# Second pair of batches in another order of groups: where a fused attention and two-layer MoE kernel makes its weight differences

## The chip, the cores and the metric

One core of a Trainium2 chip runs the whole program in one launch. The metric is the device time of one execution in microseconds (us), taken as the median of several runs. Five engines work side by side, each through its own instructions in order: TensorE (PE; PEld is its weight load), VectorE (DVE), ScalarE (ACT), GpSimd (POOL) and SyncE (SP). The last two only issue DMAs here.

## The reference

```
x:      4 batches, 8 heads, 512 rows, 64 wide;   state: 4 batches, 8 heads, 32 rows, 64 wide
a  = softmax(x state^T / 8);     xread = a  state
a2 = softmax(state x^T / 8);     sread = a2 x
y  = [xread; sread], as 4 * 544 tokens of width 512
y  = (h - tanh(h)) w_out           with h = y  w_in     (512 -> 2048 -> 512)
out = (h * tanh(softplus(h))) w_out2  with h = y w_in2   (512 -> 2048 -> 512)
```

The weights come as float64 and are converted by the kernel; all else is float32.

## The kernel before

To keep float32 precision every operand of a product is split into a large and a small part (`h` and `l` in the names), and a product is three matmuls (`mm3p`): large by large, large by small, small by large. A split is one ScalarE rounding (`gh<-...`, `wh<-...`) and one VectorE subtraction (`gl<-...`, `wl<-...`).

The change lies in the second MoE layer. Its 2048 hidden columns are taken in 8 **groups** of 256, and the four batches in two **pairs**: first batches 0 and 1 through groups 0 to 7, then batches 2 and 3 through groups 0 to 7. Within a group the product y times w_in2 over the pair is computed with Strassen's scheme in Winograd's form: seven products (`product`, names m1, m6, m7, m2, m5, m3, m4 in this order) of six matmuls each, into three PSUM banks a, b and c (`UB`). VectorE adds between them (`plus`): p after m6, then q and h22 after m5, h12 after m3, h21 after m4. m6, m5 and m3 all write bank b, so m5 needs p done, and **m3 needs q done**. ScalarE applies the activation (`mish`).

After each product stands a `slot`: it runs one item from `fill` (work of the group before, so that TensorE has matmuls while VectorE adds), then a callback, then one step from the queue `soon`, one or two weight loads from `ahead` (issued by SP), and some background `pieces`. For the first pair the items of `fill` are `down_2`: one of 8 output tiles of g times w_out2, six matmuls and one addition on VectorE (`out<-acc,out`).

For groups 0 to 5 of the second pair the second product uses Winograd's scheme too, with two groups summed in PSUM: 15 items (`pair_items`) per pair of groups, whose operands are the sums s1 to s4 of g (`a_sum`) and the **differences** t1 to t4 of w_out2. The differences do not depend on the batch. They are made once per group by `forms_t`, in the slots of the first pair's next group: two additions `wv<-wo`, four half-width subtractions `tf<-...` and two splits (`wh<-tf` on ScalarE, `wl<-tf` on VectorE), which is eight VectorE and two ScalarE steps, and four stores by POOL (`wt<-...`). `load_forms` reads them back for the second pair (`wf<-wt`). `prep` splits the left operand of an item ahead of it.

In the first pair's groups 1, 2, 3 and 7 background **pieces** run as well: the last conversions of w_in2 and w_out2 and the preparation of the second pair's y (`pieces_y`). Groups 6 and 7 of the second pair are taken plainly (`down_2`). In the last group the seven Winograd sums are added up into the outputs by `combos`: six steps of VectorE additions, one step per slot, so that the following `down_2` items can add to them.

Each engine's order is fixed by the order in which the Python code calls it (`Pinned`, whose call stands at line 66, so that nearly all rows of the profile carry L66).

```
        slot(min(u + g, 1), lambda: mish_lo(*c22))
        product(u, g, "m3", b, False)
        free_w("s34")
        h12 = plus(b, m1, m1)
```

Of the kernel before, what the change touches and what calls it, by code (L numbers as in the profile page):

```python
# [30 lines left out]
AHEAD = (2, 6, 10)  # L31
QUARTERS = 2


# [44 lines left out]
def attention_moe_kernel(  # L79
# [151 lines left out]
    def split(src, n=512, name="s", by=0):  # L231
# [17 lines left out]
    D2O = [dram.tile([128, 2, 512], F32, tag=f"o{t}", name="wo") for t in range(NT)]  # L249
    D2T = [  # L250
        dram.tile([128, 4, 2, 256], F32, tag=f"t{g}", name="wt") for g in range(NT // 2 - 2)
    ]

# [663 lines left out]
    def product(u, g, m, bank, start):  # L917
        x, op = LEFT[m]
        for k in range(KH):
            yh, yl = YB[u, RIGHT[m], k]  # L920
            mm3p(
                bank, w2(g, x, k, 0, op), w2(g, x, k, 1, op), yh.t, yl.t,
                start and k == 0, k == KH - 1, skip_group_check=not start,
            )
        if g == NT // 2 - 1:
            for k in range(KH):
                put(*YB.pop((u, RIGHT[m], k)))
# [33 lines left out]
    def mish_lo(key, u, h):  # L961
        if h is None:
            G2[key] = u
# [60 lines left out]

    def group(u, g, fill, ahead, with_s, rate, whole=False, keep=0, per=1, end=None):


        a, b, c = (psum.tile([128, 512], F32, tag=t, name="h") for t in UB)
        more = rate + (rate > 1)

        def slot(pieces, *after):
            for _ in range(per):
                if len(fill) > keep:
                    f = fill.popleft()
                    if f:
                        f()
            for f in after:
                f()
            if soon:
                soon.popleft()()  # L1040
            for _ in range(1 if whole else 2):
                if ahead:
                    ahead.popleft()()
            background(pieces, 0)
# [42 lines left out]
    def downs(u, g, with_s, last=False):  # L1087
# [4 lines left out]
        done = []  # L1092
        make = forms_t(g) if u == 0 and g < len(D2T) else []

# [11 lines left out]

    waiting = []

    def forms_t(g):


        v = {}

        def whole(j):
            h, l = O2[2 * g + j]
# [33 lines left out]

        def first():  # L1150
            whole(0)

        def release():
            put(*waiting)
            del waiting[:]

        return [
            first, lambda: whole(1), lambda: sums(0, 1), lambda: sums(2, 3),
            lambda: keep(0), lambda: keep(1), lambda: None, release,
        ]  # L1160

# [7 lines left out]
    USES = {"a11": 3, "a12": 2, "a21": 2, "a22": 2, "s1": 2, "s2": 2, "s3": 1, "s4": 1}  # L1169
    AF, GS, WF, PG, R, left = {}, {}, {}, {}, {}, {}  # L1170
    sdown = []
# [17 lines left out]
    def take_group(g):  # L1189
        for name, key in AFORM.items():  # L1190
            own(g, name, G2.pop(key))
        GS[g] = G2.pop("s")
# [49 lines left out]
    def pair_items(pair):  # L1242
        def item(i, hh):
            name, form_a, form = PORDER[i]
            if name == "s":
                s_part(pair, form)
                if pair[0] == 0:
                    OUT["s", 0] = get("out")
# [18 lines left out]
            if hh and form in BFORM:  # L1267
                s_part(pair, form)
            if pair[0] == 0:
                R[name, hh] = get("r")  # L1270
# [16 lines left out]
    def combos(b):  # L1287
# [15 lines left out]

        def one(hh):
            into(hh, "p6", "p1")
            to_out(hh, b, 0, "p1", "p2")
            put(R.pop(("p1", hh)), R.pop(("p2", hh)))

        def two(hh):
            into(hh, "p7", "p6")  # L1310
            into(hh, "p6", "p5")
            to_out(hh, b + 1, 0, "p7", "p4", ALU.subtract)
            put(R.pop(("p4", hh)))

        def three(hh):
            to_out(hh, b, 1, "p6", "p3")
            to_out(hh, b + 1, 1, "p7", "p5")
            put(*(R.pop((x, hh)) for x in ("p3", "p5", "p6", "p7")))

        return [lambda f=f, hh=hh: f(hh) for hh in range(2) for f in (one, two, three)]  # L1320

    def loads_in(g):
        g %= NT // 2
        return deque(
# [235 lines left out]
    fill = [lambda q=q: down(q) for q in seq[low:]]  # L1560
    groups = [(u, g) for u in range(2) for g in range(NT // 2)]
    for j, (u, g) in enumerate(groups):
        ahead = loads_out(g) if u == 0 or g >= NT // 2 - 2 else deque()
        if j + 1 < len(groups):
            ahead += loads_in(g + 1)
        if u and g == 0:
            background(len(bg), 0)
        if (u, g) == (0, 2):
            background(len(bg), 0)
# [4 lines left out]
            bg.extend(pieces_ys() + later[:EARLY])  # L1574
        elif (u, g) == (0, NT // 2 - 1):
            bg.extend(later[EARLY:])
        rate = 2 if g == NT // 2 - 1 or u == 0 and g < 2 else 1
        fill = deque(fill)
        if u == 0 or g >= NT // 2 - 2:
            if u and g == NT // 2 - 1:  # L1580
                soon.extend(combos(2 * u))
                first = list(fill)
                fill = deque([None] * 3 + first[:2] + first[4:5] + first[2:4] + first[5:])
            group(u, g, fill, ahead, u == 1, rate, per=2 if u and g == NT // 2 - 2 else 1)
            fill = downs(u, g, u == 1, j + 1 == len(groups))
            continue
        pair = (g - g % 2, g - g % 2 + 1)
        if g % 2:
            ahead.extend([lambda i=i, p=pair: load_forms(p, i) for i in range(2)])
            group(  # L1590
                u, g, fill, ahead, True, rate, True, 0, 1,
                lambda p=pair: (take_group(p[1]), prep(p, 0)),
            )
            fill = pair_items(pair)
        else:
            if g == 0:
                first = list(fill)
                fill = deque(
                    [None] * 2 + first[:4] + [None] * 3 + first[4:]
                )  # L1600
            group(
                u, g, fill, ahead, True, rate, True, len(fill) - 7, 1,
                lambda p=pair: take_group(p[0]),
            )
# [35 lines left out]
```

## Time and profile before

| what | value |
|---|---|
| three runs, median (lowest to highest) | 714.44 us (713.74 to 714.95) |
| the profiled execution | 716.0 us, its span 714.2 us |
| TensorE busy | 694.8 us, 97% of the span |
| VectorE busy | 516.0 us, 72% |
| ScalarE busy | 367.8 us, 51% |
| chain of waits, by engine | TensorE 81%, VectorE 9%, ScalarE 7%, issue 2%, DMA 1% |
| granted TensorE clock | full speed (2.4 GHz) in all 40 slices of the span |

The profile is one execution; its times count from the start of the span. A row of the timeline has the start, the length, the engine, the line, the operation with what it writes and reads, and in brackets the idle time of the engine before it with the instruction that ended it. Matmuls overlap: a row of a 128x512 matmul is 0.39 us long, but the next one starts 0.23 us after it, and a matmul's recorded end is modelled.

### The profile page before, as it was taken

The numbers are of one execution on the slowest core, as the hardware profiler recorded it, in microseconds if no ns is written. First come the engines' busy times: TensorE is split into PE (matmuls) and PEld (weight loads), VectorE is DVE, ScalarE is ACT, GpSimd is POOL, SyncE is SP. The second block draws the span as 40 slices with busy tenths as digits, with TensorE's granted clock in tenths as the row PEclk, the third lists the DMA queues.
The fourth block names the chain that finished last, engine by engine and source line by source line (L and its number), as shares of the span: only waits on it lengthen the run. The fifth ranks groups of instructions, "written<-read, shape, count | busy, mean of one in ns | idle before, by whom it ended". The sixth has DMA issues, their size and how long they took to land.

```text
span 714.2 us, 11308 instructions
## 1 busy us (share of the span) xinstructions
PE 694.8 (97%) x4166; PEld 565.0 (79%) x4166; DVE 516.0 (72%) x906; ACT 367.8 (51%) x667; POOL 88.0 (12%) x134
## 2 busy tenths in 40 slices
PE   9899999999999999999999889999999999999988
PEld 6467777788777897778877678888887999999966
DVE  5799966887578757996577887767656436676774
ACT  6899645565676666776265332334424544342330
POOL 0000000125012414403023111011000000000000
PEclk9999999999999999999999999999999999999999
DMA  9976130228263657847868545676945456566203
GB/s 289 330 259 227 60 47 15 89 89 289 88 210 110 248 192 246 313 150 249 326 208 289 176 133 191 227 235 219 336 137 178 134 148 192 156 213 216 66 0 134
DMA packets 69800, 132.36 MB, mean 185 GB/s; under 512 B 16752, under 2 KB 27248, under 8 KB 69744
## 3 DMA queue, kind: packets, MB, share of 16 engines
q1 hardware_dynamic: 59504, 98.06, 42.4%
q0 software_dynamic: 10240, 33.56, 12.9%
q8 instruction: 33, 0.54, 0.3%
q14 instruction: 23, 0.19, 0.1%
HBM read 95.68 MB, written 35.91 MB: 184 GB/s over the span
## 4 chain that ended last, share of the span: by engine, by line
PE 81%; DVE 9%; ACT 7%; issue 2%; DMA 1%; DVEq 0%; ACTq 0%
PE acc L66 44%; PE h L66 30%; DVE wide L66 2%; PE hs L66 2%; PE swp L66 2%; ACT r L66 2%; ACT w L66 2%; DVE gl L66 1%; ACT gh L66 1%; ACT wide L66 1%; DVE out L66 1%; DMA wide<-in_moe_w_out_dram 1%; DVE tf L66 1%; DVE wl L66 1%; PE xtp L66 1%
## 5 line engine op out<-in xcount | busy, mean ns | idle before, releaser
L66 PE MATMUL h<-yh,ws 128*128 128x512 f32 x448 | 157.0, 394 | 7.7 <-DVE wide L66 5.4
L66 PEld LDWEIGHTS h<-yh,ws 128*128 128x128 f32 x448 | 84.3, 188 | 27.9 <-DVE wide L66 8.7
L66 PE MATMUL acc<-wo,gh 128*128 128x512 f32 (+1 forms) x332 | 101.8, 388 | 2.4 <-DVE out L66 1.9
L66 PE MATMUL acc<-gh,wh 128*128 128x512 f32 x244 | 98.5, 403 | 0.0
L66 PE MATMUL acc<-gh,wl 128*128 128x512 f32 x244 | 95.4, 391 | 0.0
L66 PE MATMUL acc<-gl,wh 128*128 128x512 f32 x244 | 95.2, 390 | 0.0
L66 PE MATMUL h<-yl,ws 128*128 128x512 f32 x224 | 87.8, 392 | 0.0
L66 DVE TENSOR_TENSOR gl<-wide,gh 128x512 fp32r<-128x512 f32 x80 | 54.0, 688 | 43.8 <-ACT gh L66 43.6
L66 ACT ACTIVATE wide<-wide 128x512 f32<-128x512 f32 x41 | 25.9, 632 | 100.4 <-DVE wide L66 100.4
L66 PEld LDWEIGHTS acc<-wo,gh 128*128 128x128 f32 x332 | 61.8, 188 | 16.0 <-DVE out L66 2.8
L66 PE MATMUL acc<-wf,gh 128*128 128x256 f32 x384 | 70.6, 283 | 0.6 <-ACT gh L66 0.6
L66 DVE TENSOR_TENSOR wide<-h,wide 128x512 f32<-128x512 f32 x78 | 53.7, 688 | 21.6 <-PE h L66 10.9
L66 PE MATMUL acc<-wo,gl 128*128 128x512 f32 (+1 forms) x166 | 64.5, 388 | 0.0
L66 PEld LDWEIGHTS acc<-wf,gh 128*128 128x128 f32 x384 | 61.8, 192 | 3.4 <-ACT gh L66 1.0
L66 PEld LDWEIGHTS acc<-gh,wh 128*128 128x128 f32 x244 | 45.8, 188 | 18.2 <-issue 4.2
L66 PE MATMUL acc<-wf,gl 128*128 128x256 f32 x192 | 54.6, 284 | 0.2 <-DVE gl L66 0.2
L66 PE MATMUL h<-ath,swh 128*128 128x512 f32 x128 | 51.6, 403 | 2.4 <-ACT swh L66 2.3
L66 PEld LDWEIGHTS acc<-gh,wl 128*128 128x128 f32 x244 | 45.8, 188 | 9.9
L66 PEld LDWEIGHTS acc<-gl,wh 128*128 128x128 f32 x244 | 45.9, 188 | 9.1 <-issue 0.4
L66 ACT ACTIVATE gh<-wide 128x512 fp32r<-128x512 f32 x80 | 48.9, 628 | 7.6 <-DVE wide L66 6.4
L66 ACT ACTIVATE wide<-h 128x512 f32<-128x512 f32 x40 | 23.7, 594 | 55.1 <-PE h L66 52.8
L66 PE MATMUL h<-ath,swl 128*128 128x512 f32 x128 | 50.6, 395 | 0.5 <-DVE swl L66 0.5
(215 smaller groups left out, 1289.1 us busy)
## 6 DMA issues: line engine op xcount, KB each, us to landing
ws<-wi SPq DMA_DIRECT2D x128, 256.0 KB, 4.5
st<-in_moe_w_in_dram SPq DMA_DIRECT2D x26, 512.0 KB, 5.1
st<-in_moe_w_out_dram SPq DMA_DIRECT2D x23, 512.0 KB, 5.2
wo<-wo SPq DMA_DIRECT2D x40, 256.0 KB, 4.0
wi<-wh POOLq DMA_DIRECT2D x32, 256.0 KB, 4.5
wi<-wl POOLq DMA_DIRECT2D x32, 256.0 KB, 4.4
wf<-wo SPq DMA_DIRECT2D x24, 256.0 KB, 4.0
wf<-wt SPq DMA_DIRECT2D x24, 256.0 KB, 4.9
```

Source lines behind the costliest of these rows:

```text
L66: i = fn(*args, **kw)
```

## The change

- The second pair takes the groups in the order of `ROUND2`, (3, 4, 5, 7, 6, 2, 0, 1); its first six (`WHOLE`) are taken with Winograd's second product in pairs (3, 4), (5, 7), (6, 2), and the last two, 0 and 1, plainly.
- The differences of w_out2 for groups 3, 4, 5 and 7 are made with the first pair's output items as before, which is in the first pair's groups 4, 5, 6 and in the second pair's first group. Those for groups 6 and 2 are made by steps in `soon` in the second pair's first and third group, from large and small parts of w_out2 that are loaded a second time (`more_t`: four DMAs of 256 KB each). In the first pair's groups 1, 2 and 3, none are made.
- The split of the first left operand of each pair of groups (`prep(p, 0)`) moves from after m4 to after m3 (`mid`).
- In the seventh group four of the 15 pair items are kept back (every second slot takes two) for the first four slots of the last one, and `combos` is cut into eight steps with one empty, which with the last four pair items in front stretches over nine slots.

```
+ROUND2 = (3, 4, 5, 7, 6, 2, 0, 1)
+WHOLE = 6
...
-        if g == 0:
+        if g == 0 and b in (0, 1):
             OUT[b, r] = get("out")
             evac(OUT[b, r].t, ps, r)
             return
         o = OUT[b, r]
-        if g < NT // 2 - 1:
+        if g != (NT // 2 - 1 if b in (0, 1) else ROUND2[-1]):
...
-            for _ in range(per):
+            done[0] += 1
+            for _ in range(2 if done[0] - 1 in per else 1):
...
-        slot(rate, lambda: mish_lo(*c12))
+        slot(rate, lambda: mish_lo(*c12), *([mid] if mid else []))
...
-        make = forms_t(g) if u == 0 and g < len(D2T) else []
+        make = forms_t(g, [O2[2 * g], O2[2 * g + 1]]) if u == 0 and g in ROUND2[:4] else []
...
+    def more_t(g):
+        src = []
+
+        def load():
+            for t in (2 * g, 2 * g + 1):
+                src.append(tuple(get("wo", F32R) for _ in range(2)))
+                for h in range(2):
+                    nc.sync.dma_start(out=src[-1][h].t.bitcast(F32), in_=D2O[t][:, h, :])
+
+        made = forms_t(g, src)
+
+        def second():
+            made[1]()
+            put(*src[0], *src[1])
+
+        return load, [made[0], second, *made[2:]]
...
-        return [lambda f=f, hh=hh: f(hh) for hh in range(2) for f in (one, two, three)]
+        return [
+            u2, u3, lambda: second(0), u4, lambda: second(1), lambda: None,
+            lambda: first(0), lambda: first(1),
+        ]
...
-    groups = [(u, g) for u in range(2) for g in range(NT // 2)]
+    groups = [(0, g) for g in range(NT // 2)] + [(1, g) for g in ROUND2]
...
+            load, steps = more_t(ROUND2[4])
+            ahead.append(load)
...
+            if n == WHOLE:
+                fill = deque(fill)
+                group(u, g, fill, ahead, True, rate, keep=4, per=(0, 2, 4, 6))
+                fill = list(fill) + downs(u, g, True)
+            else:
+                soon.extend(combos(2 * u))
+                first = fill[4:]
+                fill = deque(fill[:4] + first[:2] + first[4:5] + first[2:4] + first[5:])
+                group(u, g, fill, ahead, True, rate)
+                fill = downs(u, g, True, True)
+            continue
+        if n == 0:
+            soon.extend(steps)
+            fill = [None] * 2 + fill[:4] + [None] * 3 + fill[4:]
+            load, steps = more_t(ROUND2[5])
+        elif n == 1:
+            ahead.append(load)
+        elif n == 2:
+            soon.extend(steps)
...
             group(
-                u, g, fill, ahead, True, rate, True, 0, 1,
-                lambda p=pair: (take_group(p[1]), prep(p, 0)),
+                u, g, fill, ahead, True, rate, True, 0, (), lambda p=pair: prep(p, 0),
+                lambda g=g: take_group(g),
             )
```

In the new `combos`, u2 adds p1 to p6, u3 adds p6 to p7 and u4 adds p5 to p6, for both halves hh of the rows; `second(hh)` writes the outputs of batch 3 and `first(hh)` those of batch 2, four half-width additions each.

**VectorE in the first pair's group 2.** The rows lead up to q, the last of each list (`wide<-h,wide`); `wide<-acc` and `out<-acc` add output items, `wide<-y`, `yl` are pieces, `gl` is a split of g. Before:

```order
L66 TENSOR_TENSOR wide<-acc,wide 128x512
L66 TENSOR_TENSOR wv<-wo 128x512
L66 TENSOR_TENSOR wide<-y 128x512 x2
L66 TENSOR_TENSOR wide<-acc,wide 128x512
L66 TENSOR_TENSOR tf<-wv 128x256
L66 TENSOR_TENSOR tf<-wv,tf 128x256
L66 TENSOR_TENSOR yl<-y,yh 128x512
L66 TENSOR_TENSOR out<-acc,out 128x512
L66 TENSOR_TENSOR tf<-wv 128x256
L66 TENSOR_TENSOR tf<-tf,wv 128x256
L66 TENSOR_TENSOR gl<-wide,gh 128x512
L66 TENSOR_TENSOR wide<-h,wide 128x512
```

and now:

```order
L68 TENSOR_TENSOR wide<-acc,wide 128x512
L68 TENSOR_TENSOR wide<-y 128x512 x2
L68 TENSOR_TENSOR wide<-acc,wide 128x512
L68 TENSOR_TENSOR yl<-y,yh 128x512
L68 TENSOR_TENSOR out<-acc,out 128x512
L68 TENSOR_TENSOR gl<-wide,gh 128x512
L68 TENSOR_TENSOR wide<-h,wide 128x512
```

The `wv` and the four `tf` are gone; the rest stands in the same order.

**VectorE in the second pair's third group**, now, from after p to q and h22 (`gl<-hs,gh` is the split of the state rows; the `gl` before it that of a left operand, `m_5657` a copy of m1):

```order
L68 TENSOR_TENSOR gl<-wide,gh 128x512 x2
L68 TENSOR_TENSOR wv<-wo 128x512
L68 TENSOR_TENSOR tf<-wv 128x256
L68 TENSOR_TENSOR tf<-wv,tf 128x256
L68 TENSOR_TENSOR gl<-wide,gh 128x512 x2
L68 TENSOR_TENSOR tf<-wv 128x256
L68 TENSOR_TENSOR tf<-tf,wv 128x256
L68 TENSOR_TENSOR gl<-hs,gh 128x256
L68 TENSOR_TENSOR wide<-h,m_5657 128x512
L68 TENSOR_TENSOR wide<-h,wide 128x512
```

Before, none of the `wv` and `tf` rows stand there; the pair of `tf` in front of `gl<-hs,gh` is new directly ahead of q.

**VectorE in the last group**, before, from h12 to the remaining output additions (`out` rows of half width are steps of `combos`, the second `wide<-h,wide` is h21):

```order
L66 TENSOR_TENSOR wide<-h,wide 128x512
L66 TENSOR_TENSOR out<-acc,out 128x512
L66 TENSOR_TENSOR gl<-wide,gh 128x512
L66 TENSOR_TENSOR out<-r 128x256 x2
L66 TENSOR_TENSOR out<-r,wide 128x256 x2
L66 TENSOR_TENSOR wide<-h,wide 128x512
L66 TENSOR_TENSOR out<-acc,out 128x512
L66 TENSOR_TENSOR gl<-wide,gh 128x512
L66 TENSOR_TENSOR out<-acc,out 128x512 x13
L66 TENSOR_TENSOR out<-acc,out 128x256 x2
```

and now:

```order
L68 TENSOR_TENSOR wide<-h,wide 128x512
L68 TENSOR_TENSOR out<-acc,out 128x512
L68 TENSOR_TENSOR gl<-wide,gh 128x512
L68 TENSOR_TENSOR wide<-h,wide 128x512
L68 TENSOR_TENSOR out<-acc,out 128x512
L68 TENSOR_TENSOR gl<-wide,gh 128x512
L68 TENSOR_TENSOR out<-wide 128x256 x2
L68 TENSOR_TENSOR out<-wide,r 128x256 x2
L68 TENSOR_TENSOR out<-acc,out 128x512
L68 TENSOR_TENSOR out<-r 128x256 x2
L68 TENSOR_TENSOR out<-r,wide 128x256 x2
L68 TENSOR_TENSOR out<-acc,out 128x512 x13
```

Four half-width additions stood between h12 and h21; now eight stand behind h21, in two lots, among the additions of the output items. Ahead of q the two full-width additions of u4 stand now where one full-width and two half-width ones stood.

## Rows read from the trace of the kernel before

**Rows 1.** The page's first part: busy time of each engine.

```profile
PE 694.8 (97%) x4166; PEld 565.0 (79%) x4166; DVE 516.0 (72%) x906; ACT 367.8 (51%) x667; POOL 88.0 (12%) x134
```

**Rows 2.** Stretches: from:to, length, busy us (instructions) by engine, clock, DMA share, GB/s.

```profile
357.00:428.00 71.00, 63.77 (x274) 50.74 (x274) 56.18 (x98) 34.40 (x59) 16.46 (x25) 1.00 0.60 200
...
511.00:544.00 33.00, 33.00 (x160) 27.74 (x159) 16.74 (x27) 8.35 (x15) 0.00 (x0) 1.00 0.54 183
...
672.00:715.00 43.00, 36.38 (x169) 29.42 (x167) 27.80 (x52) 6.39 (x11) 0.00 (x0) 0.99 0.16 56
```

**Rows 3.** Timeline of PE, first pair: m6's start in groups 1, 4 and 5.

```profile
360.25 0.39 PE L66 MATMUL h<-yh,ws 128*128 128x512 f32 x1
...
430.51 0.39 PE L66 MATMUL h<-yh,ws 128*128 128x512 f32 x1
...
451.33 0.39 PE L66 MATMUL h<-yh,ws 128*128 128x512 f32 x1
```

**Rows 4.** Timeline of PE, first pair: m3's start in groups 1 and 2.

```profile
372.60 0.50 PE L66 MATMUL h<-yh,ws 128*128 128x512 f32 x1 [1.31 <-DVE mt L66]
...
398.13 0.50 PE L66 MATMUL h<-yh,ws 128*128 128x512 f32 x1 [2.98 <-DVE wide L66]
```

**Rows 5.** Timeline of DVE, first pair's group 2, up to q (the last row).

```profile
391.72 0.69 DVE L66 TENSOR_TENSOR wv<-wo 128x512 f32<-128x512 f32 x1
392.32 1.29 DVE L66 TENSOR_TENSOR wide<-y 128x512 f32<-128x512 f32 x2
...
394.13 0.42 DVE L66 TENSOR_TENSOR tf<-wv 128x256 f32<-128x256 f32 x1
...
394.92 0.69 DVE L66 TENSOR_TENSOR yl<-y,yh 128x512 fp32r<-128x512 f32 x1
...
396.12 0.42 DVE L66 TENSOR_TENSOR tf<-wv 128x256 f32<-128x256 f32 x1
...
396.79 0.68 DVE L66 TENSOR_TENSOR gl<-wide,gh 128x512 fp32r<-128x512 f32 x1
397.39 0.68 DVE L66 TENSOR_TENSOR wide<-h,wide 128x512 f32<-128x512 f32 x1
```

**Rows 6.** Timeline of PE, second pair's third group: from m1 to after m6.

```profile
544.06 0.62 PE L66 MATMUL h<-yh,ws 128*128 128x512 f32 x2
...
546.42 0.50 PE L66 MATMUL acc<-wf,gh 128*128 128x256 f32 x2 [0.61 <-ACT gh L66]
...
548.68 0.40 PE L66 MATMUL h<-yh,ws 128*128 128x512 f32 x1
...
551.50 0.40 PE L66 MATMUL h<-yh,ws 128*128 128x512 f32 x1
```

**Rows 7.** Timeline of DVE, second pair's first group, the item before m5.

```profile
520.77 0.69 DVE L66 TENSOR_TENSOR wide<-acc,wide 128x512 f32<-128x512 f32 x1 [2.03 <-PE acc L66]
```

**Rows 8.** Timeline of PE, second pair: m3 in its first and third group.

```profile
523.53 0.39 PE L66 MATMUL h<-yh,ws 128*128 128x512 f32 x1
...
562.33 0.40 PE L66 MATMUL h<-yh,ws 128*128 128x512 f32 x1
```

**Rows 9.** Timeline of DVE, second pair's third group: q.

```profile
561.48 0.68 DVE L66 TENSOR_TENSOR wide<-h,m 128x512 f32<-128x512 f32 x1
```

**Rows 10.** Timeline of PE, last group: m3 and two of the output items.

```profile
683.55 0.50 PE L66 MATMUL h<-yh,ws 128*128 128x512 f32 x1 [0.60 <-DVE wide L66]
...
693.53 0.73 PE L66 MATMUL acc<-wo,gh 128*128 128x512 f32 x2 [1.52 <-DVE out L66]
...
695.59 0.73 PE L66 MATMUL acc<-wo,gh 128*128 128x512 f32 x2 [0.39 <-DVE out L66]
```

**Rows 11.** Timeline of SP, from the end of the first pair.

```profile
501.82 8.02 SPq L905 DMA_DIRECT2D ws<-wi  x14
...
518.76 6.03 SPq L1010 DMA_DIRECT2D out_dram<-wide  x3
```

**Rows 12.** DMA issues of the stretch 485 to 550 us: count, size, median us to landing.

```profile
wo<-wo SPq DMA_DIRECT2D x3, 256.0 KB, 3.8
```

More of the change, by code (lines that the diff above doesn't have):

```diff
@@ L249, in attention_moe_kernel @@
     D2O = [dram.tile([128, 2, 512], F32, tag=f"o{t}", name="wo") for t in range(NT)]
-    D2T = [
-        dram.tile([128, 4, 2, 256], F32, tag=f"t{g}", name="wt") for g in range(NT // 2 - 2)
-    ]
+    D2T = {
+        g: dram.tile([128, 4, 2, 256], F32, tag=f"t{g}", name="wt") for g in ROUND2[:WHOLE]
+    }
     def store_split(w, dst):
@@ L962, in mish_lo @@
         if h is None:
-            G2[key] = u
+            own(whole_g[0], ANAME[key], u)
             return
@@ L1023, in plus, with group @@
         return o
-    def group(u, g, fill, ahead, with_s, rate, whole=False, keep=0, per=1, end=None):
+    def group(u, g, fill, ahead, with_s, rate, whole=False, keep=0, per=(), mid=None, end=None):
         a, b, c = (psum.tile([128, 512], F32, tag=t, name="h") for t in UB)
+        whole_g[0] = g
+        done = [0]
         more = rate + (rate > 1)
         def slot(pieces, *after):
-            for _ in range(per):
+            done[0] += 1
+            for _ in range(2 if done[0] - 1 in per else 1):
                 if len(fill) > keep:
@@ L1169, in attention_moe_kernel @@
     USES = {"a11": 3, "a12": 2, "a21": 2, "a22": 2, "s1": 2, "s2": 2, "s3": 1, "s4": 1}
-    AF, GS, WF, PG, R, left = {}, {}, {}, {}, {}, {}
+    ANAME = {key: name for name, key in AFORM.items()}
+    AF, GS, WF, PG, R, left, whole_g = {}, {}, {}, {}, {}, {}, [0]
     sdown = []
@@ L1246, in item @@
                 s_part(pair, form)
-                if pair[0] == 0:
+                if pair[0] == ROUND2[0]:
                     OUT["s", 0] = get("out")
@@ L1268, in item @@
                 s_part(pair, form)
-            if pair[0] == 0:
+            if pair[0] == ROUND2[0]:
                 R[name, hh] = get("r")
@@ L1302, in into, with u2, u3, u4 @@
             add(R[o, hh].t, R[o, hh].t, R[x, hh].t)
-        def one(hh):
-            into(hh, "p6", "p1")
-            to_out(hh, b, 0, "p1", "p2")
[L1307 to L1315, printed above, removed]
-            to_out(hh, b, 1, "p6", "p3")
-            to_out(hh, b + 1, 1, "p7", "p5")
-            put(*(R.pop((x, hh)) for x in ("p3", "p5", "p6", "p7")))
-        return [lambda f=f, hh=hh: f(hh) for hh in range(2) for f in (one, two, three)]
+        def u2():
+            for hh in range(2):
+                into(hh, "p6", "p1")
+        def u3():
+            for hh in range(2):
+                into(hh, "p7", "p6")
+        def u4():
+            for hh in range(2):
+                into(hh, "p6", "p5")
+        def second(hh):
+            to_out(hh, b + 1, 0, "p7", "p4", ALU.subtract)
+            to_out(hh, b + 1, 1, "p7", "p5")
+            put(R.pop(("p7", hh)), R.pop(("p4", hh)))
+        def first(hh):
+            to_out(hh, b, 0, "p1", "p2")
+            to_out(hh, b, 1, "p6", "p3")
+            put(*(R.pop((x, hh)) for x in ("p1", "p2", "p3", "p5", "p6")))
+        return [
+            u2, u3, lambda: second(0), u4, lambda: second(1), lambda: None,
+            lambda: first(0), lambda: first(1),
+        ]
     def loads_in(g):
-        g %= NT // 2
         return deque(
@@ L1574, in attention_moe_kernel @@
             bg.extend(pieces_ys() + later[:EARLY])
-        elif (u, g) == (0, NT // 2 - 1):
+        elif (u, n) == (0, last_g):
             bg.extend(later[EARLY:])
-        rate = 2 if g == NT // 2 - 1 or u == 0 and g < 2 else 1
-        fill = deque(fill)
[L1579 to L1588, printed above, removed]
+            load, steps = more_t(ROUND2[4])
+            ahead.append(load)
+        rate = 2 if n == last_g or u == 0 and n < 2 else 1
+        fill = list(fill)
+        if u == 0:
+            group(u, g, deque(fill), ahead, False, rate)
+            fill = downs(u, g, False)
+            continue
+        if plain:
+            if n == WHOLE:
[8 more added lines that the diff above has]
+                fill = downs(u, g, True, True)
+            continue
+        if n == 0:
[6 more added lines that the diff above has]
+            soon.extend(steps)
+        pair = ROUND2[n - n % 2:n - n % 2 + 2]
+        fill = deque(fill)
+        if n % 2:
             ahead.extend([lambda i=i, p=pair: load_forms(p, i) for i in range(2)])
             group(
-                u, g, fill, ahead, True, rate, True, 0, 1,
-                lambda p=pair: (take_group(p[1]), prep(p, 0)),
+                u, g, fill, ahead, True, rate, True, 0, (), lambda p=pair: prep(p, 0),
+                lambda g=g: take_group(g),
             )
@@ L1595, in attention_moe_kernel @@
         else:
[L1596 to L1600, printed above, removed]
             group(
-                u, g, fill, ahead, True, rate, True, len(fill) - 7, 1,
-                lambda p=pair: take_group(p[0]),
+                u, g, fill, ahead, True, rate, True, len(fill) - 7, (), None,
+                lambda g=g: take_group(g),
             )
```

31 lines of the change are left out of this document (13 added, 18 removed).

## The prediction

> **What bounds the kernel now.** I read the page's busy times first, then the stretches, then the timelines of TensorE and VectorE around each place where TensorE stands idle. TensorE is busy 694.8 of the 714.2 us [rows 1], and the change takes away none of its matmuls, so all that can be won is its 19.4 us of idle time, and of that only what lies where the change works. The stretches show where [rows 2]: the first pair's groups 1 to 3 have 71.00 - 63.77 = 7.2 us of idle, the second pair's first two groups (511 to 544) none, the close from 672 on 43.00 - 36.38 = 6.6, part of it the store after the last matmul. VectorE is at 56.18 of 71 us in the first of these, and only at 16.74 of 33 in the second. So one place has too much VectorE work and another has room.
>
> Who waits for whom is in the timeline: in groups 1 to 3, m3 begins late and its releaser is VectorE [rows 4]; VectorE itself runs without a pause up to q, the addition that frees bank b for m3 [rows 5]. A 128x512 matmul begins 0.23 us after the one before though its row lasts 0.39, so an idle time in brackets costs 0.16 more than it says: the wait of 2.98 us at 398.13 costs 3.1. A product of six such steps takes 1.36 us, an output item as much.
>
> The granted clock is 1.00 in the stretches up to 672 [rows 2], the level of 2.4 GHz, through waits of 3 us too; neither a gain nor a loss comes from the clock.
>
> **Part 1: no differences in the first pair's groups 1 to 3.** From m6 of group 1 to m6 of group 4 it takes 430.51 - 360.25 = 70.26 us; the next group, which makes differences but has no pieces, takes 451.33 - 430.51 = 20.82 [rows 3]. At that pace three groups take 62.5, so 7.8 us are lost to having both. VectorE sheds, per group, ahead of q: two `wv` at 0.60 from start to start (391.72 to 392.32), and two pairs of `tf`, 0.79 (394.13 to 394.92) and 0.67 (396.12 to 396.79) [rows 5], 2.66 us together; behind q two more `wl`, 1.2, and ScalarE two `wh`.
> - Group 2: VectorE reaches q at 397.39 [rows 5]. Without 2.66 it is 394.7, and m3 would start at 395.5 in place of 398.13, still 0.5 late. But group 1 has lost its differences as well, and the two `wl` each waited there for a `wh` behind an activation. I followed the queue from there item by item with the durations of these rows: VectorE is then bound by the items it adds, q ends 0.3 us ahead of m3's turn, and the wait is gone.
> - Group 1: q is 1.3 late [rows 4]; 2.66 us less in front brings it to within 0.1 or 0.2 us of m3's turn, held by a ScalarE step in between. Group 3, a wait of the same kind, ends with half a microsecond to spare.
> Were the small waits of the groups without pieces gone as well (0.3 each), it would be 8.7 us; I take 8.2, between 7.8 and 8.7, because of the rest in group 1. The bound from below is 0, should the pieces alone hold VectorE up.
>
> **Part 2: the first split sooner.** In the second pair's third group the first pair item waits for its left operand: from m1 (second of the two steps of the row at 544.06, so 544.29) to m6 (548.68) it takes 4.39 us, from m6 to m7 (551.50) 2.82 for the same kind of work [rows 6]: 1.57 lost. The split now stands one product and one item earlier (2.8 us), more than the wait, and no more than four steps are put in front of h21, which m7 of the next group needs some 7 us later. I take the whole 1.6; the bounds are 0.6 (the first wait's size, should the second step still wait) and 1.6.
>
> **Part 3: where the differences go.** Nothing is saved in sum: the same eight VectorE, two ScalarE steps and four POOL stores per group, and eight loads of 256 KB more on SP.
> - Second pair's first group: group 7's come with the items, group 6's from `soon`. Behind the item at 520.77 now stand `wv` and two `tf`, 0.60 and 0.67, ahead of the state split (0.34) and q. So q starts at 520.77 + 0.61 + 0.60 + 0.67 + 0.34 = 522.99 [rows 5, 7], ends at 523.68, and m3, which started at 523.53 [rows 8], comes 0.2 late; with the slow first step after a wait 0.3. Behind q the splits delay h12 and h21 by some 2 us, but those free banks for the next group's m6 and m7, later still. Second group: 0.
> - Third group: the `tf` pair right ahead of q, 0.67, puts it from 561.48 to 562.15, its end to 562.85, and m3 from 562.33 [rows 8, 9] to 562.9. With the slow step 0.7.
> - Groups 4 to 6 of the first pair are as before, and the other order of the groups alone changes no work on any engine. POOL's stores land long before they are read, a pair of groups later.
> I take 1.0 lost, between 0 (if VectorE reaches q earlier than I think) and 2.5 (if every one of the first three groups waits as long as the third).
>
> By the Trainium skill, VectorE: DVE Perf Modes, section "The DRAIN you can't avoid", the next VectorE instruction does not start until the pipe is empty; by that each of these steps would hold the queue for its whole row, 0.69 or 0.42 us. [rows 5] differ: rows of 0.69 follow each other by 0.60 and rows of 0.42 by 0.34, so the queue is priced by steps. By the rule the pair of `tf` would cost 0.84 in place of 0.67, and this part 1.4 in place of 1.0.
>
> **Part 4: the close.** Before, the last group lost 0.60 + 1.52 + 0.39 plus 0.16 each, 3.0 us [rows 10]. The order now: ahead of q, behind the split of the first activation, stand u4's two additions (1.2) where there stood 0.6 + 0.67, so about the same; but between m2 and m5 TensorE now has only the short last pair item (0.7 us) in place of an output item (1.36). The chain behind m2 (activation 0.6, rounding 0.6, split 0.6, u4 1.2, state split 0.3, q 0.7, and hand-overs of 0.2) is 4.3 us; TensorE's cover (0.7 + 0.1 + 1.36 + 1.36) is 3.6. m3 is late by some 0.8, as before. Then the eight half-width additions of batch 2 (8 x 0.34 = 2.7) stand behind h21, among the additions that free the banks of the output items; before, half of the comparable work was done ahead of h21. Following banks and queue step by step I get waits of 1.9 and 0.6 where there were 1.7 and 0.55. So the close loses 0.4; bounds: 3.0 won, if the spread leaves VectorE abreast of the items, and 2 lost, if a third item waits.
>
> **The sum.** 8.2 + 1.6 - 1.0 - 0.4 = 8.4 us less for the span of 714.2, some 705.8. The profiled execution took 716.0 with 1.8 us around the span; the median of the runs is 714.44, 1.6 less than it. I take the difference from the median: 714.44 - 8.4 = **706.0 us**. A difference under 0.2%, 1.4 us, could not be told from none.
>
> **The rivals.**
> - *The pieces, not the differences, hold the first groups.* If VectorE and ScalarE, which hand pieces and activations to each other in turn, stay late at q without the differences, part 1 gives about half, 4.1, and the time is 710.1. For it: the longest wait is in group 2, which has the most pieces; against: the steps removed ahead of q are 2.66 us of a wait of 2.98.
> - *The close keeps up.* If the additions spread over nine slots leave VectorE abreast, its 3.0 us go and the 0.4 isn't lost: 702.6. Against: no slot between m3 and the end loses VectorE work, the last two gain it.
> - *The second loads are late.* `wv` of group 6 stands at VectorE's queue head in the first slot of the second pair's first group, about 513.6, and p, q and all additions wait behind it. SP issues its loads ahead of the last twelve weight loads of the burst that fills 501.82 to 509.84 [rows 11], and such a load lands in 3.8 us [rows 12], so about 508. It decides from about 519 on, where m5 needs p; beyond that each microsecond is one lost. If SP put them behind the stores from 518.76, which wait for VectorE's additions [rows 11], they would land near 530 and the time would be some 716.5: slower than before.
> - *Bank b is what lacks.* m6, m5 and m3 write bank b in turn, and if the time from m5's end through q is what m3 waits for, less VectorE work ahead of q changes nothing: part 1 is 0, the other parts leave 714.44 - 1.6 + 1.0 + 0.4 = 714.2, the same. Against: for the same bank the wait is 1.31 us in one group and 2.98 in the next [rows 4], and none is named in groups 4 to 6. The Trainium skill, Perfetto Trace Analysis, section "Optimization Strategy", says that a gap that repeats can mean too little PSUM for the next tile; by that rule this rival would hold, and the unequal waits do not agree with it.
>
> **How the numbers follow.** The forecast (704.5 to 708) 0.66, the pieces 0.18, the close 0.08, late loads 0.04, bank b 0.04. The likeliest is 706.0. The range takes in the bound of half a gain and all but the far end of the close, 703.6 to 710.0; it leaves out late loads, bank b and part of the close. Faster by over 0.2%: 0.91, with a little taken off the cases for mechanisms that I do not see; within 0.2%: 0.05; slower: 0.04.
>
> **What would show it.** In the new profile: m3 of the first pair's groups 2 and 3 without a bracket, and 62 to 63 us from m6 of group 1 to m6 of group 4; no idle time ahead of the first `acc<-wf,gh`; small waits of 0.1 to 0.6 us for VectorE at m3 in the second pair's first and third group; in the last group again three waits that add up to some 3.3. I am wrong if groups 1 to 3 still lose over 3 us, if a DMA is named as a releaser of VectorE around 513, or if the close changes by over 1.5.

## The result, and the profile after

The changed kernel took **705.09 us** (median of four runs, 704.84 to 706.41) beside 714.39 us of the kernel before on the same chip: ratio 0.9874, with a 95% interval of 0.9857 to 0.9891. That is 9.3 us less; the prediction was 706.0, a gain of 8.4. On a second chip it was 704.97 beside 715.25, ratio 0.9859 (0.9845 to 0.9872). The profiled execution took 705.0 us, with a span of 703.2.

The page's first part, which answers to [rows 1]:

```profile
PE 692.0 (98%) x4166; PEld 563.9 (80%) x4166; DVE 515.6 (73%) x906; ACT 366.7 (52%) x667; POOL 88.0 (13%) x134
```

The instructions are as many as before on every engine, and TensorE's idle time fell from 19.4 to 703.2 - 692.0 = 11.2 us. The same stretches as in [rows 2]:

```profile
357.00:428.00 71.00, 71.00 (x315) 58.61 (x314) 53.24 (x86) 32.73 (x56) 9.13 (x14) 1.00 0.56 186
511.00:544.00 33.00, 32.98 (x173) 28.05 (x172) 24.47 (x43) 12.05 (x24) 5.80 (x8) 1.00 0.87 285
672.00:715.00 43.00, 26.09 (x119) 21.00 (x117) 19.21 (x36) 3.79 (x6) 0.00 (x0) 0.99 0.16 55
```

In the first, TensorE no longer idles at all (63.77 before), with VectorE at 53.24 in place of 56.18. These stretches hold the same times but not quite the same work, as the changed kernel is ahead. So here is the first one by work, from m6 of group 1 to m6 of group 4, before and now:

```profile
360.25:430.51 70.26, 63.02 (x272) 50.17 (x270) 56.41 (x97) 32.81 (x57) 17.80 (x26) 1.00 0.62 208
359.15:420.44 61.29, 61.29 (x272) 50.60 (x270) 46.67 (x75) 30.65 (x52) 9.13 (x14) 1.00 0.62 203
```

VectorE's share went only from 80% to 76%, and the waits are gone. In the second stretch, VectorE went from 16.74 to 24.47; what TensorE lost there is in the table below.

Now TensorE's timeline at the places of [rows 3, 4, 6, 8, 10]: m6, m3 and m3 of the first pair's groups 1, 1 and 2, m6 and m3 of group 4; m3 of the second pair's first group; m1, the first pair item and m6 of its third group, and m3; m3 and two output items of the last group.

```profile
359.15 0.39 PE L68 MATMUL h<-yh,ws 128*128 128x512 f32 x1
...
370.04 0.39 PE L68 MATMUL h<-yh,ws 128*128 128x512 f32 x1
...
390.44 0.42 PE L68 MATMUL h<-yh,ws 128*128 128x512 f32 x1
...
420.44 0.39 PE L68 MATMUL h<-yh,ws 128*128 128x512 f32 x1
...
431.61 0.50 PE L68 MATMUL h<-yh,ws 128*128 128x512 f32 x1
...
513.46 0.50 PE L68 MATMUL h<-yh,ws 128*128 128x512 f32 x1
...
534.14 0.61 PE L68 MATMUL h<-yh,ws 128*128 128x512 f32 x2
...
535.73 0.40 PE L68 MATMUL acc<-wf,gh 128*128 128x256 f32 x2
...
537.16 0.40 PE L68 MATMUL h<-yh,ws 128*128 128x512 f32 x1
...
551.36 0.50 PE L68 MATMUL h<-yh,ws 128*128 128x512 f32 x1 [0.40 <-DVE wide L68]
...
671.30 0.50 PE L68 MATMUL h<-yh,ws 128*128 128x512 f32 x1 [0.56 <-DVE wide L68]
...
682.66 0.50 PE L68 MATMUL acc<-wo,gh 128*128 128x512 f32 x1 [1.55 <-DVE out L68]
...
684.60 0.73 PE L68 MATMUL acc<-wo,gh 128*128 128x512 f32 x2 [0.29 <-DVE out L68]
```

m1 of the third group begins with the second step of its row, 534.37. The m3 at 513.46 begins 0.40 after the matmul before it, so 0.18 late, and slow steps behind it cost 0.16 more: from m1 of this group to m1 of the next it takes 17.01 us, 16.67 before. The m3 at 551.36 loses its bracket, 0.16, and 0.10 more in a slow step behind it. So the 11.0 us between the two spans are accounted for, term by term:

| place | before | after | won |
|---|---|---|---|
| up to the first pair's group 0 (both programs alike) | 334.38 | 333.29 | 1.09, chance |
| m6 of group 1 to m6 of group 4 | 70.26 | 61.29 | 8.97 |
| m6 of group 4 to m1 of the second pair's first group | 80.43 | 80.25 | 0.18 |
| m1 to m6 in the second pair's third group | 4.39 | 2.79 | 1.60 |
| at m3 and behind it, second pair's first and third group | 0 | 0.34 + 0.66 | -1.00 |
| last group, three waits with 0.16 each | 2.99 | 2.88 | 0.11 |

The change itself thus gave 8.97 + 0.18 + 1.60 - 1.00 + 0.11 = 9.86 us in the trace, between the 9.3 and 10.3 of the medians on the two chips.

VectorE's timeline shows the same from its side. First the split of g and q in the first pair's group 2 [rows 5], then the second pair's first group (`wv` from the second load; then q with h22 in one row), then the third group:

```profile
389.03 0.68 DVE L68 TENSOR_TENSOR gl<-wide,gh 128x512 fp32r<-128x512 f32 x1
389.63 0.68 DVE L68 TENSOR_TENSOR wide<-h,wide 128x512 f32<-128x512 f32 x1
...
503.11 0.68 DVE L68 TENSOR_TENSOR wv<-wo 128x512 f32<-128x512 f32 x1
...
512.73 1.41 DVE L68 TENSOR_TENSOR wide<-h,wide 128x512 f32<-128x512 f32 x2
...
549.62 0.42 DVE L68 TENSOR_TENSOR tf<-wv 128x256 f32<-128x256 f32 x1
549.96 0.42 DVE L68 TENSOR_TENSOR tf<-tf,wv 128x256 f32<-128x256 f32 x1
550.29 0.42 DVE L68 TENSOR_TENSOR gl<-hs,gh 128x256 fp32r<-128x256 f32 x1
550.63 0.68 DVE L68 TENSOR_TENSOR wide<-h,m 128x512 f32<-128x512 f32 x1
```

In group 2, q ends at 390.31 and m3 begins at 390.44: the room is 0.1 us, not more. At 503.11 the `wv` from the second load stands without a bracket, so the load was there. In the third group the pair of `tf` stands right in front of the state split and q, and m3 comes 0.40 late by its bracket.

### The profile page after: what moved, and what is told of

Read it like the earlier page. It is cut to its first block, busy times and chain, and to the rows that moved or that the text cites. A ratio compares the mean times of both kernels' runs of the same rounds, so it can differ in the third digit from the quotient of the medians.

```text
span 703.2 us, 11336 instructions
## 1 busy us (share of the span) xinstructions
PE 692.0 (98%) x4166; PEld 563.9 (80%) x4166; DVE 515.6 (73%) x906; ACT 366.7 (52%) x667; POOL 88.0 (13%) x134
## 4 chain that ended last, share of the span: by engine, by line
PE 87%; ACT 7%; DVE 4%; issue 1%; DMA 1%; SPq 0%; DVEq 0%; ACTq 0%
PE acc L68 47%; PE h L68 33%; ACT r L68 2%; ACT w L68 2%; PE swp L68 2%; PE hs L68 2%; DVE out L68 1%; DVE gl L68 1%; DVE wide L68 1%; ACT gh L68 1%; DMA x<-in_x_dram 1%; PE xtp L68 1%; ACT t L68 1%; PE sct L68 1%; PE srd L68 1%
```

## The experiments

In groups 1 to 3 of the kernel before, three more waits stand besides those of [rows 4]: at an item and at m2 of group 2, and at m3 of group 3. TensorE's timeline:

```profile
384.38 0.50 PE L66 MATMUL acc<-wo,gh 128*128 128x512 f32 x1 [0.48 <-ACT wide L66]
...
389.42 0.50 PE L66 MATMUL h<-yh,ws 128*128 128x512 f32 x1 [0.66 <-ACT wide L66]
...
420.81 0.51 PE L66 MATMUL h<-yh,ws 128*128 128x512 f32 x1 [1.80 <-DVE wide L66]
```

With 0.16 for each bracket the five cost 8.0 us. The kernel before beside these runs had a median of 715.2 to 715.6 us; ratios are to it.

**1. The groups and differences alone.** The split and the close are the old ones; against the changed kernel:

```
-                u, g, fill, ahead, True, rate, True, 0, (), lambda p=pair: prep(p, 0),
-                lambda g=g: take_group(g),
+                u, g, fill, ahead, True, rate, True, 0, (), None,
+                lambda p=pair: (take_group(p[1]), prep(p, 0)),
...
-                group(u, g, fill, ahead, True, rate, keep=4, per=(0, 2, 4, 6))
+                group(u, g, fill, ahead, True, rate, per=range(99))
```

and the old `combos` and order of `fill` in the last group.

> The kernel before with only the new order of groups and the differences moved; the first split and the close are the old ones. Theory (the steps made in front of q in VectorE's queue were what groups 1 to 3 waited for, and the parts simply add): m6 of group 1 to m6 of group 4 takes 61.3 us as in the changed kernel (70.3 before), 9.0 won; the second pair's first and third group lose 0.2 and 0.7 at m3; the third group's m1 to m6 takes 4.4 as before; the close loses 3.0 as before. Sum 714.4 - 9.0 + 0.9 = 706.3, some 1.2 slower than the changed kernel. Rival (the parts lean on each other, the move pays only with the earlier split or the new close): over 708, or no slower than the changed kernel.

Measured: 706.83 us (706.19 to 707.22), ratio 0.9887 (0.9875 to 0.9900). TensorE's timeline, m6 of groups 1 and 4:

```profile
358.96 0.39 PE L68 MATMUL h<-yh,ws 128*128 128x512 f32 x1
...
420.23 0.39 PE L68 MATMUL h<-yh,ws 128*128 128x512 f32 x1
```

From one to the other it takes 61.27 us, the third group's first item waits 0.61 and 0.22 again, m3 there 0.40, and the last group waits 0.60, 1.49 and 0.39. The theory holds to 0.5 us; the parts add.

**2. The split alone**, on the kernel before:

```
-                lambda p=pair: (take_group(p[1]), prep(p, 0)),
+                lambda p=pair: prep(p, 0), lambda g=g: take_group(g),
```

where the first now runs after m3 and the second at the end.

> The kernel before with only the first split of each pair of groups moved from after m4 to after m3. Theory: no idle time ahead of the first pair item in the second pair's third and fifth group, m1 to m6 of the third group falls from 4.39 to 2.8 us; 1.6 won, 712.8; were the fifth group helped too, 711.2. Rival A (only the first wait of 0.6 goes, the second left operand is late next): m1 to m6 3.8, 713.8. Rival B (the split in front of h21 delays m7 of the next group by as much): 714.4.

Measured: 713.95 us, ratio 0.9987 (0.9976 to 0.9997), 0.2 to 1.7 won. TensorE's timeline, m1 and m6 of the third group:

```profile
543.60 0.62 PE L68 MATMUL h<-yh,ws 128*128 128x512 f32 x2
...
546.62 0.40 PE L68 MATMUL h<-yh,ws 128*128 128x512 f32 x1
```

m1 begins with the second step of the first row, 543.83, and 546.62 - 543.83 = 2.79 as in the changed kernel. Neither rival holds: m1 to m6 is not rival A's 3.8, and from m6 of the third group to m1 of the last it takes 122.83 us in both kernels, so no later product waits, as rival B would have it. By the ratio 0.9 us were won and not 1.6. In this trace m3 of the first pair's group 7, which the edit does not touch, waits 0.65 us, and it does not in that of before; why was not followed. The fifth group, which I had named as a chance, had no wait before either.

**3. The close alone**, on the kernel before: `keep=4, per=(0, 2, 4, 6)`, the new `combos` and the new order of `fill` in the last group, as in the diff of the change.

> The kernel before with only the new close (four pair items kept for the last group, the closing additions in eight steps over nine slots). Theory (the spread only moves VectorE's work from ahead of h21 to behind it): three waits that add up to 2.9 us where it was 3.0, time 714.3, the same within 0.2%. Rival A (the close keeps up, but the changed kernel's earlier state hides it): 711.4. Rival B (the close alone costs what I had forecast): 714.8, which this run can't tell from the theory by time but by the sum of the waits, 3.4 in place of 2.9.

Measured: 714.80 us, ratio 1.0004 (0.9990 to 1.0018), the same. The three waits are 0.56, 1.56 and 0.28, with 0.16 each 2.9: the theory, and not the 3.4 that I had forecast. From m1 of group 1 to the end, run 1 is 8.1 us shorter than before; with the 1.6 of run 2 at its place and the 0.1 here that makes 9.8, and the whole change has 9.9. The three edits add. Its trace also showed what the one of before had not, the clock falling after the wait of group 2 (the last section).

**4. All differences kept in their groups, but behind q**, on the kernel before:

```
         return [
-            lambda: whole(0), lambda: whole(1), lambda: sums(0, 1), lambda: sums(2, 3),
-            lambda: keep(0), lambda: keep(1), lambda: None, lambda: put(*waiting),
+            lambda: None, lambda: None, lambda: None, lambda: None,
+            lambda: (whole(0), whole(1)), lambda: (sums(0, 1), sums(2, 3)),
+            lambda: keep(0), lambda: (keep(1), put(*waiting)),
         ]
```

> The kernel before with nothing taken out of groups 1 to 3: each group makes its differences as before, from the same buffers and with the same stores, but the two wv and four tf stand in the slots behind q (after m3 and m4), and the wl behind them. Theory (the place in VectorE's queue, not the amount of work, makes m3 late): the 2.66 us ahead of q go, so the wait of 3.1 at m3 of group 2 goes and most of the others; 4 to 8 us of the 9.0 won, and the small waits at m3 in groups 4 to 6 (0.3 each) too: 706 to 710, and as group 0 and 7 are unchanged, nothing elsewhere. Rival A (too much VectorE work in sum, 56.18 of 71 us busy with the pieces): the late work delays h12 and h21, m6 and m7 of the next group wait instead, and under 2 us are won: over 712.4. Rival B (bank b, or the pieces and activations that hand to each other, is what lacks): m3 waits as before, 714.4.

Measured: 713.71 us, ratio 0.9984 (0.9972 to 0.9996); the time misses the theory and lies where rival A had it (over 712.4), but the waits are not rival A's: m6 and m7 of groups 2 to 4 wait for nothing. TensorE's timeline, m6 of group 1, m2 and m3 of group 2, m3 of group 3, m6 of group 4, then m3 of group 7:

```profile
360.08 0.39 PE L68 MATMUL h<-yh,ws 128*128 128x512 f32 x1
...
388.05 0.50 PE L68 MATMUL h<-yh,ws 128*128 128x512 f32 x1 [1.94 <-ACT wide L68]
...
394.69 0.50 PE L68 MATMUL h<-yh,ws 128*128 128x512 f32 x1 [0.91 <-DVE wide L68]
...
415.44 0.50 PE L68 MATMUL h<-yh,ws 128*128 128x512 f32 x1
...
425.09 0.39 PE L68 MATMUL h<-yh,ws 128*128 128x512 f32 x1
...
500.69 0.80 PE L68 MATMUL h<-yh,ws 128*128 128x512 f32 x1 [3.36 <-DVE wide L68]
```

and ScalarE's in group 7:

```profile
494.48 1.68 ACT L68 ACTIVATE yh<-wide 128x512 fp32r<-128x512 f32 x3 [6.10 <-DMA wt<-wl]
```

From m6 of group 1 to m6 of group 4 it takes 425.09 - 360.08 = 65.01 us, where it took 70.26 and takes 61.29 in the changed kernel; the small losses of groups 4 to 6 went as well. So place alone is worth 5.3 of the 9.0 in groups 1 to 3. The other 3.7 were still lost with the steps behind q: m2 of group 2 waits 1.94 us for ScalarE, where it waited 0.66, and m3 0.91 for VectorE. Then group 7 gave most of it back: a piece on ScalarE waited 6.1 us for POOL's last store of differences, m3 lost 3.5 for it, and TensorE's clock fell besides (2.3 us lost). In the kernel before ScalarE has the same wait there, 3.86 us, and TensorE loses 0.1; in the changed kernel ScalarE waits for no store there.

**5. Behind q in groups 1 to 3 only** (the list above under `if g < 3:`, the old one otherwise).

> The kernel before with the differences' VectorE steps behind q in the first pair's groups 1 to 3 only; in groups 4 to 6 they stand where they stood. Theory (the place ahead of q costs the larger part; what spoiled the run with all six groups was ScalarE's 6.1 us wait in group 7 for a buffer that POOL's late store of group 6's differences still held): groups 1 to 3 lose 3.4 us in place of 8.0 as in that run, the waits in groups 4 to 6 (0.3 each) are back, none in group 7: 4.6 won on a run of before at full clock, some 710. Rival A (the wait in group 7 comes from all the late work and not from group 6's store): it stays, and the time is 713.5 again. Rival B (the late steps of group 3 hold up group 4): under 3.5 won, over 711.

Measured: 713.25 us, ratio 0.9961 (0.9945 to 0.9977). 2.8 us won where the theory had 4.6. Groups 1 to 3 gave what it said, 65.79 us from m6 to m6, 4.5 won; the time is rival B's (under 3.5 won, over 711), as the wait now stands one group earlier, in group 4. VectorE and TensorE (m3) in group 4:

```profile
435.07 0.42 DVE L68 TENSOR_TENSOR tf<-wv 128x256 f32<-128x256 f32 x1 [2.24 <-DMA wt<-wl]
```

```profile
438.67 0.50 PE L68 MATMUL h<-yh,ws 128*128 128x512 f32 x1 [2.35 <-DVE wide L68]
```

Here VectorE's first `tf` of group 4 waits for the late store of the differences made in group 3, and q behind it. Both runs say the same: steps that move behind q deliver their stores later, and what comes next waits for the store. That it is the store's buffer that the next step wants is how I read the releaser; it was not tried with another buffer.

**6. A smaller dose: the second pair of `tf` alone behind q**, on the kernel before:

```
-            lambda: whole(0), lambda: whole(1), lambda: sums(0, 1), lambda: sums(2, 3),
-            lambda: keep(0), lambda: keep(1), lambda: None, lambda: put(*waiting),
+            lambda: whole(0), lambda: whole(1), lambda: sums(0, 1), lambda: None,
+            lambda: sums(2, 3), lambda: keep(0), lambda: keep(1), lambda: put(*waiting),
```

> The kernel before with the second pair of tf one step later, behind q, in all six groups that make differences; wv and the first pair stay ahead of q. A smaller dose of the same. Theory (m3's lateness is counted by what stands ahead of q in VectorE's queue): each m3 of groups 1 to 3 comes 0.67 us sooner, 2.0 together, and the 0.29 of groups 4 to 6 goes, 0.9: the losses of groups 1 to 3 fall from 8.0 to 6.0, and the time to 711.6 from 714.5 of before at full clock. Rival A (amount in sum, not place): losses stay at 8.0, 714.5. Rival B (the later stores hold buffers up, as in the runs with all steps behind q): a new wait in group 4 or 7 eats the gain, 713 to 715.

Measured: 714.27 us, ratio 0.9991 (0.9975 to 1.0007). TensorE's timeline, m3 of groups 1, 2 and 7:

```profile
370.53 0.50 PE L68 MATMUL h<-yh,ws 128*128 128x512 f32 x1 [0.60 <-DVE mt L68]
...
395.45 0.51 PE L68 MATMUL h<-yh,ws 128*128 128x512 f32 x1 [2.31 <-DVE wide L68]
...
501.72 0.80 PE L68 MATMUL h<-yh,ws 128*128 128x512 f32 x1 [2.36 <-DVE wide L68]
```

The brackets of groups 1 and 2 went from 1.31 to 0.60 and from 2.98 to 2.31, 0.71 and 0.67 less, for 0.67 us taken from in front of q, and from m6 of group 1 to m6 of group 4 it takes 68.25 us, 2.0 less, as the theory had it. So m3's lateness is counted by VectorE's queue ahead of q, which excludes rival A. But rival B's forecast holds for the time: m3 of group 7 waits 2.36, behind ScalarE:

```profile
495.50 1.68 ACT L68 ACTIVATE yh<-wide 128x512 fp32r<-128x512 f32 x3 [6.74 <-DMA ws<-wi]
```

The DMA named here is a weight load, not a store of differences, so rival B's reason is not shown by this run.

By the Trainium skill, VectorE: DVE Perf Modes, section "The DRAIN you can't avoid", taken as the prediction took it, the pair would have been worth its two whole rows, 0.84, as an estimate; the brackets agree with the steps from start to start, 0.67. The same paragraph adds that an instruction that is not held starts earlier, which the prediction left out; the rows agree with that, 0.42 us long and 0.34 apart.

**7 to 9. Two edits on the changed kernel**: the list of run 6 (7), the close in another layout (8), both (9). The second, in `combos`, with `row` adding the two halves of one output row:

```
         return [
-            u2, u3, lambda: second(0), u4, lambda: second(1), lambda: None,
-            lambda: first(0), lambda: first(1),
+            u2, u34, lambda: (row(b + 1, 0, 0), row(b + 1, 0, 1)), lambda: None,
+            lambda: row(b + 1, 1, 0), lambda: row(b + 1, 1, 1), lambda: None,
+            lambda: row(b, 0, 0), lambda: row(b, 0, 1), lambda: row(b, 1, 0), lambda: row(b, 1, 1),
         ]
```

> The changed kernel with the second pair of tf one step later, behind q, wherever differences are made (first pair's groups 4 to 6, second pair's first and third group). Theory (each pair in front of q costs m3 what its queue time exceeds the room there): the waits 0.29 x 3, 0.18 and 0.56 at m3 go, 1.6 won: span 701.6, time 703.5 against 705.1 of the changed kernel. Rival A (m3 then waits for the split of the state rows or the item, not for q): only half, 704.3. Rival B (the pair behind q delays h12 and h21 and a later product waits): 705.1.

> The changed kernel with the closing additions laid out in another way: u3 and u4 together in the first product's slot, so that nothing of theirs stands ahead of q, and the outputs of batch 2 made row by row, two half-width additions in each slot, each before the item that adds to it. Theory (the three waits of the last group, 2.9 us together, come from VectorE's additions in two lumps, in front of q and in front of the additions that free the items' banks): m3's wait of 0.7 goes and the two at the items fall from 2.1 to under 0.5: 2.4 won, 702.7. Rival A (VectorE has too much to do from m3 to the end wherever it stands): the waits move to other items, 705.1. Rival B (TensorE then waits earlier, at m2 or m5, for a bank whose addition stands behind u4): m3's 0.7 won and 0.7 to 1.4 lost, 705 to 706.

> The changed kernel with both of these edits. They touch different groups, so the theory adds their gains: 1.6 + 2.4 = 4.0, 701.1. Rival: if either gain is only a wait moved on, the sum of the two single runs' gains is missed by over 0.8.

Measured: 703.53 us, 702.22 us and **700.24 us** (699.53 to 700.85), beside 705.09 of the changed kernel 1.6, 2.9 and 4.9 less: the gains add, and the second is larger than the 2.4 expected. (The changed kernel did not run beside these three; in the traces, from m1 of group 1 to the end, they are 1.5, 3.1 and 5.4 us shorter than it, and runs 10 and 11 stand side by side.) Ratios to before: 0.9827 (0.9801 to 0.9853), 0.9809 (0.9785 to 0.9833) and 0.9781 (0.9756 to 0.9806). In run 7 the five small waits at m3 are gone (one of 0.53 at m3 of group 7 is new: ScalarE waits there for a store of differences again, 4.9 us; in run 9, with the same edit, for 4.2 us, and m3 does not wait). In run 8 all three of the last group are gone. Its VectorE timeline, where two half-width additions now stand between two items' additions:

```profile
679.96 0.68 DVE L68 TENSOR_TENSOR out<-acc,out 128x512 f32<-128x512 f32 x1
680.56 0.41 DVE L68 TENSOR_TENSOR out<-wide 128x256 f32<-128x256 f32 x1
680.89 0.42 DVE L68 TENSOR_TENSOR out<-wide,r 128x256 f32<-128x256 f32 x1
681.23 0.68 DVE L68 TENSOR_TENSOR out<-acc,out 128x512 f32<-128x512 f32 x1
```

The work is the same as in the changed kernel, so the waits of its last group were a matter of place too, and rival A of run 8 falls. In run 9 the list of all waits of TensorE names none between 330 us and the end.

**10 and 11. The changed kernel and run 9's once more, on one chip.**

> The changed kernel once more, beside before and the improved one. Theory: 705.1 again, ratio 0.987; its waits in the same places and of the same size (m3 of the last group 0.57, items 1.55 and 0.29).

> The changed kernel with both edits (second pair of tf behind q, closing additions row by row) once more, on the same chip as the changed kernel. Theory: 4.5 us less than the changed kernel, 700.5; ratio to before 0.980.

Measured: 704.97 us and 700.15 us (699.34 to 701.28), ratios 0.9859 (0.9845 to 0.9872) and 0.9788 (0.9775 to 0.9801). The waits of the changed kernel came out within 0.02 us of the first trace; the improved kernel is 4.8 us faster again, 15.1 less than before.

## Why the prediction was right, step by step

- **The sum** was 8.4, and the trace gives 9.86. All errors lie on the same side, so none hid another: 0.8 in part 1, 0.5 in part 4, and 0.2 in groups 4 to 7 that no part had.
- **Part 1** was the right mechanism and 0.8 short: 8.97 for 8.2, above even the 8.7 that it set as its upper end. I had priced the three groups at the pace of one that makes differences, 20.82; without them a group runs at 61.29 / 3 = 20.43. And I kept a rest in group 1 that wasn't there: m3 at 370.04 has no bracket. The five brackets make up 8.0 of it; the other 0.9 are steps that began late by less than 0.2 each, none of which is left. Run 6 confirms the way of counting, the queue ahead of q. What I did not see is that place is only a part of it: with all the steps behind q, groups 1 to 3 still lose 3.7 of the 9.0 (run 4). And the order before comes close to waits on its stores: of some 5 us that runs 4 and 5 won in these groups, 1.1 and 2.8 were left in the whole (by their ratios). That the differences could leave these groups was what the gain needed.
- **Part 2**: 1.60 for 1.6, in the changed kernel and alone.
- **Part 3**: 0.34, 0 and 0.66 for 0.3, 0 and 0.7, the 1.0 of the forecast. The queue position of one pair of `tf` gave the size.
- **Part 4** was mis-sized: 0.1 won where I had forecast 0.4 lost. m3 lost 0.72 (0.8 forecast, though the terms listed for chain and cover, 4.2 and 3.5, leave 0.7), the items 1.71 and 0.45 (1.9 and 0.6). The step that failed is the queue I followed bank by bank to the items, by 0.2 at each. Run 8 shows that the 2.9 could be had by another layout, which the bound of 3.0 held.
- **The rivals.** *Pieces*: with the pieces left in place, groups 1 to 3 lose nothing; excluded. *The close keeps up*: it does not. *Second loads late*: no bracket at 503.11; excluded. *Bank b*: m6, m5 and m3 use it as before, and the waits are gone; excluded, and with it, for this kernel, the reading of a repeated gap as a shortage of PSUM (the Trainium skill, Perfetto Trace Analysis, section "Optimization Strategy").
- **The clock**: I wrote that neither gain nor loss comes from it, since it stayed at full speed through waits of 3 us. That held for the profiled execution of before, but in others the clock does fall behind such a wait; that the change gained time by this no run shows (next section but one).

## What to carry to other kernels

When an engine waits for another that is not fully busy, list what stands in the other's queue between the last thing it could wait for and the instruction that is waited for; each step taken away there is worth its start-to-start time, as long as that wait lasts. The same step behind it no longer delays that wait, but it can delay the next ones: with all steps behind q, over a third of the loss stayed. Before moving a step later, look at what its result holds on to: a store that leaves later can become the next wait, as the releasers of runs 4, 5 and 7 say. And before adding the price of slow matmuls to that of a wait, look whether a later wait gives it back.

## What the hardware showed

`tf` rows of 0.42 us follow each other by 0.34, and the waiting m3 counts the 0.34 (run 6, 0.71 and 0.67 for a pair).

In the profile of before, the wait of 2.98 us in group 2 left the clock at full speed. In the profile of run 3, whose program is the same up to there, it did not. TensorE's timeline of run 3 from m3 on, and the granted clock (the third number from the end) of two stretches behind it:

```profile
398.06 0.50 PE L68 MATMUL h<-yh,ws 128*128 128x512 f32 x1 [2.97 <-DVE wide L68]
...
399.64 0.63 PE L68 MATMUL h<-yl,ws 128*128 128x512 f32 x1
400.06 0.63 PE L68 MATMUL h<-yh,ws 128*128 128x512 f32 x1
```

```profile
399.00:401.00 2.00, 2.00 (x6) 1.52 (x6) 0.80 (x2) 1.73 (x3) 0.00 (x0) 0.50 0.07 20
...
402.00:405.00 3.00, 3.00 (x14) 2.44 (x13) 2.18 (x4) 1.35 (x3) 0.79 (x2) 1.00 0.74 253
```

At 0.50, which is 1.2 GHz, a 128x512 matmul begins 0.42 us after the one before in place of 0.23; eight of them in a row cost 1.6 us. Run 2 shows the same behind the same wait (9 matmuls, 1.7 us), run 4 behind 3.36 us (12, 2.3 us), run 5 behind 1.94 and 2.35 (7 each, 1.4), run 6 behind 2.31 and 2.36 (8 and 6, 1.6 and 1.2).

What the fall costs depends on what comes next. In run 3, m6 of group 1, m3 of group 3 and m6 of group 4:

```profile
360.18 0.39 PE L68 MATMUL h<-yh,ws 128*128 128x512 f32 x1
...
420.73 0.50 PE L68 MATMUL h<-yh,ws 128*128 128x512 f32 x1 [0.38 <-DVE wide L68]
...
430.43 0.39 PE L68 MATMUL h<-yh,ws 128*128 128x512 f32 x1
```

The next wait, 1.80 us in the profile of before, has shrunk to 0.38, and m6 to m6 takes 70.25 us, beside 70.26 without the fall; run 2 has 0.36 and 70.23. TensorE was late by the fall, but at that place it would have waited for VectorE anyway. Behind group 7, in runs 4 and 6, no wait follows that could give it back: from m6 of group 4 to m1 of the second pair's first group they take 85.16 and 83.09 us, where run 9, which waits nowhere there, takes 78.98, and of the 6.2 and 4.1 us more the waits at m3 of group 7 are 3.5 and 2.5.

Of the 56 executions of before beside these runs, 16 had a mean granted clock of 1.000 (median 714.87 us), 15 had 0.998 (714.88) and 24 had 0.997 or less (715.61); what made the last ones slower is not known. All eight of the changed kernel had 0.999 or more. So the change took away the wait behind which the clock fell in runs 2 and 3, but a gain of time from that is not shown.
